# A float64 weight conversion in an attention and MLP kernel: from two byte-shifted loads to one load and integer steps

## The chip, the cores and the metric

The kernel runs on one core of a Trainium2 chip. The metric is the device time of one execution in microseconds; the profile's times come from one execution taken by the hardware profiler. A core has TensorE (PE: matmuls, and PEld for its weight loads), VectorE (DVE), ScalarE (ACT), GpSimd (POOL) and SyncE (SP, which here only starts transfers), each with its own queue of instructions in a fixed order, and 16 DMA engines that all queues share.

## The reference

Attention over 8 batches of 8 heads (576 rows of 64 numbers each, float32), in which scores more than tau below their row's largest are dropped, and then a two-layer MLP with an exact GELU over the 4608 rows of 512:

```python
scores = scale * np.matmul(q, k.transpose(0, 1, 3, 2))
thresh = np.max(scores, axis=-1, keepdims=True) - tau
scores = np.where(scores >= thresh, scores, -1000000000.0)
scores = scores - np.max(scores, axis=-1, keepdims=True)
attn = np.exp(scores)
attn = attn / (np.sum(attn, axis=-1, keepdims=True) + 1e-09)
x = np.matmul(attn, v)          # then (B,H,S,D) -> (B*S, H*D)
...
h = x @ w_in                    # 512 x 2048
g = 0.5 * h * (1.0 + erf(h * inv_sqrt2))
return (g @ w_out).astype(np.float32)   # 2048 x 512
```

q, k and v are float32. The two weights are float64: each number arrives as two 32-bit words, and the kernel has to make float32 of 2 x 1,048,576 of them.

## The kernel before

**Stages.** The kernel goes through 32 pairs of heads (`NP`), four pairs to a batch, and five chunks of query rows to a pair. One step of its main loop (line 845) takes one pair and one chunk; I call it a slot. The first batch is the early phase, slots 0 to 19: its list of slots (line 817) first takes chunks 0 and 1 of all four pairs, then chunks 2, 3 and 4 of each. Chunks 0 to 3 have two score tiles of 128 x 576, chunk 4 (the tails of both heads) has one. In the early phase PE also turns q and k (`turn_qk_early`) and the softmax output (`turn_p_early`) by matmuls, later DVE's transposes and DMAs do that. Behind the attention, PE fills in MLP blocks of 256 rows (`fill`, `block_steps`): layer one is L559, layer two L573. The last ten blocks are done at the end in five pairs by a Strassen scheme (L693).

**One early slot, in the order of the engines' queues.** PE makes the scores sc (L367), which need the two PSUM buffers that the slot before has freed. DVE finds the negative row maximum nmx (L379), POOL makes the threshold thr (L380), ACT the exponentials p (L382). DVE then masks p and sums it (L398). Conversion steps of the weights come next on DVE and ACT. POOL adds 1e-9 to the sums (L401). At the end of the slot DVE inverts them (den, L409), and ACT writes them on a diagonal, diag (L412). In the next slot PE multiplies p with diag (tr, L309), which divides and turns at once, and ACT copies the result out (pT, L317, L328; L321 and L333 for chunk 4). PE's xT (L484) weighs v with pT, and ACT copies that too (L493). Every second early slot up to slot 4 also has ACT copy the turned q and k (L283, L285, L292, L293, L296). From slot 10 on, PE does some 10 or 12 records of layer one (hT, L559) between scores and tr.

**The weights** are 32 pieces of 128 x 512 numbers, 16 of w_in and 16 of w_out. `load_piece` (line 139) starts the DMAs of one piece, twice: the piece as it is (raw, L156: 1024 words a row) and the same bytes moved by three (shifted, L158), so that a shifted word has the 28 bits of the number's fraction in place. Even pieces and the last two go to tiles of the pool xg, odd ones to the tile turned_p, which is idle in the early phase. Two pieces are started on SP before the loop (line 810), one each in slots 0 and 2 (line 891); after that each conversion that ends starts the next load, on POOL's queue.

`conversions` (line 161) is a generator that gives out the steps of a piece, and its yields are the nanoseconds that a step is counted as. For each piece: DVE masks the exponent bits (L177), ACT scales and rebiases them into a float32 power of two (L178), DVE cuts the fraction out of the shifted words (L185), puts the sign to the power (L187), and multiplies both (L189). The first two steps run one piece ahead. `convert(ns)` (line 196) runs steps until their yields have used up what it was given: nothing in slot 0, 2000 in slots 1 and 2, 3800 in each further slot of the early phase (line 910), and some of it between nmx and p (line 876). The last two pieces wait until the others are done.

Of the kernel before, what the change touches and what calls it, by code (L numbers as in the profile page):

```python
# [8 lines left out]
FP32 = mybir.dt.float32  # L9
U32 = mybir.dt.uint32  # L10
U8 = mybir.dt.uint8
AF = mybir.ActivationFunctionType
ALU = mybir.AluOpType
# [5 lines left out]
def kernel(  # L19
# [28 lines left out]
    nc = tc.nc  # L48
# [4 lines left out]
    P = 128  # L53
# [24 lines left out]
    const = ctx.enter_context(tc.tile_pool(name="const", bufs=1))  # L78
# [4 lines left out]
    xg = ctx.enter_context(tc.tile_pool(name="xg", bufs=7))  # L83
    op = ctx.enter_context(tc.tile_pool(name="op", bufs=2))
# [17 lines left out]
    pd = [turned_p[:, e, :, :, :].rearrange("p h b i -> p (h b i)") for e in range(2)]  # L102
# [8 lines left out]
    q_scale = const.tile([P, 1], FP32, name="q_scale")  # L111
    tau_eff = const.tile([P, 1], FP32, name="tau_eff")

    rebias = const.tile([P, 1], FP32, name="rebias")
    nc.vector.memset(rebias, -8.0 * 896 * 2 ** 20)

    w_in_sb = [const.tile([P, d_ff], FP32, name=f"w_in{c}") for c in range(N_DM)]
    w_out_sb = [const.tile([P, d_model], FP32, name=f"w_out{j}") for j in range(N_DF)]

# [4 lines left out]
    for _ in range(3):  # L124
# [3 lines left out]
    PIECE = 512  # L128
    pieces = [(w_in_sb[c][:, f:f + PIECE], moe_w_in[c * P:(c + 1) * P, f:f + PIECE])
              for f in range(0, d_ff, PIECE) for c in range(N_DM)]  # L130
# [3 lines left out]
    LATER = 2  # L134
    raws = []
    loaded = [0]
    converted = [0]

    def load_piece(eng=nc.gpsimd):
        if loaded[0] == len(pieces):  # L140
            return
        dst, src = pieces[loaded[0]]
        loaded[0] += 1
        if not wide:
            nc.sync.dma_start(dst, src)
            converted[0] += 1
            load_piece()
            return
        k = loaded[0] - 1
        if k % 2 and k < len(pieces) - LATER:  # L150

            room = pd[k // 2 % 2].bitcast(U32)
            raw, shifted = room[:, 0:2 * PIECE], room[:, 2 * PIECE:4 * PIECE]
        else:
            raw, shifted = (xg.tile([P, 2 * PIECE], U32, tag="x", name=s) for s in ("raw", "shifted"))
        eng.dma_start(raw, src.bitcast(U32))  # L156
        n = 8 * PIECE - 4
        eng.dma_start(shifted.bitcast(U8)[:, 0:n], src.bitcast(U8)[:, 3:3 + n])  # L158
        raws.append((dst, raw, shifted))

    def conversions():

        vec = nc.vector
        ahead = []  # L170
        while raws or ahead:
            if raws:
                dst, raw, shifted = raws.pop(0)
                hi = raw.rearrange("p (f w) -> p f w", w=2)[:, :, 1]
                top = shifted.rearrange("p (f w) -> p f w", w=2)[:, :, 0]
                power = gp.tile([P, PIECE], U32, tag="g", name="power")
                vec.tensor_scalar(power, hi, 0x7FF00000, None, op0=ALU.bitwise_and)  # L177
                nc.scalar.activation(power, power, AF.Relu, bias=rebias, scale=8.0)  # L178
                ahead.append((dst, hi, top, dst.bitcast(U32), power))
                yield 340  # L180
            if len(ahead) == LATER and converted[0] == len(pieces) - LATER:
                yield None
            if len(ahead) == 2 or not raws:
                dst, hi, top, mant, power = ahead.pop(0)
                vec.tensor_scalar(mant, top, 0x0FFFFFFF, 0x10000000, op0=ALU.bitwise_and, op1=ALU.bitwise_or)  # L185
                yield 340
                vec.scalar_tensor_tensor(power, hi, 0x80000000, power, op0=ALU.bitwise_and, op1=ALU.bitwise_or)  # L187
                yield 720
                vec.scalar_tensor_tensor(dst, mant, 2.0 ** -28, power.bitcast(FP32), op0=ALU.mult, op1=ALU.mult)  # L189
                load_piece()  # L190
                converted[0] += 1
                yield 700

    conv = {"steps": None, "debt": 0.0}

# [162 lines left out]
    def scores(p, i):  # L358
        s = st[p]
        n = 1 if i == NC else 2  # L360
        sc = s["sc", i] = [ps.tile([P, 2, 512], FP32, tag="sc", name="sc", bufs=2) for _ in range(n)]
        for h in range(2):
            for e in range(n):
                rows = slice(0, P) if i == NC else slice(e * D, (e + 1) * D)
                lhsT = s["q_tail"] if i == NC else s["qT"][rows, i * P:(i + 1) * P]
                at = h * HALF + (TAIL if p < EARLY and e == 0 else 0)
                nc.tensor.matmul(  # L367
                    sc[e][:, h, 0:HALF], lhsT=lhsT, rhs=s["kT"][rows, at:at + HALF], start=True, stop=True)
# [150 lines left out]
    def gelus(left):  # L519


        while len(late) > left:
            g, j, hT = late.pop(0)
            t = gp.tile([P, 2, TOK], FP32, tag="g", name="g")
            if hold[0]:
                nc.scalar.copy(t, hT)
                held.append((g, j, t))
            else:
                gelu(g, j, t, hT)
# [82 lines left out]
    vec = nc.vector  # L612
# [193 lines left out]
    load_early(2)  # L806
    for t in q_tail + v_sb:
        nc.gpsimd.memset(t, 0.0)
    for _ in range(2):
        load_piece(nc.sync)  # L810
    turn_qk_early(0)
    load_v_early(0)
# [32 lines left out]
    for n in range(len(slots) + WEIGH + 1):  # L845
        p, i = slots[n] if n < len(slots) else divmod(n, SLOTS)
        early = p < EARLY
        last = slots[n - 1] if 0 < n <= len(slots) else None
        if p < NP:
            scores(p, i)  # L850
            softmax_head(p, i)
            if p < HP - 1 and i == 0:
                turn_qk_early(p + 1)
        elif n == len(slots):
            ext = weights_in()
        gelus(0)
        if n == BATCH:
            gelus_held()
        table()
        for args in due:  # L860
            weigh_v(*args)
        due = []
        if p > EARLY and i == WEIGH:
            for lo, hi in (0, WIDE), (WIDE, S):
                weigh_v(p - 1, lo, hi)
            if p == NP:
                divide(p - 1)
        owed += (goal(n) - goal(n - 1)) * BLK_NS * (PARTS[i] if not early and p < NP else 1.0)
        if early:
            fill(owed, tokens)  # L870
            owed = 0.0
            table()
        if last and last[0] < EARLY and last[1] < NC:
            turn_p_early(*last)
        if early and n > 2:
            convert(0, 700 if i == NC else 1)
        if p < NP:
            softmax_tail(p, i)
        if p < NP and not early:
            turn_p(p, i)  # L880
        if p < NP and not early:
            if i == 2:
                regroup(p, 1)
            if i > 2:
                regroup(p, i)
            if i == NC:
                divisors(p)
        if last and last[0] < EARLY and last[1] == NC:
            turn_p_early(*last)
        if p < 2 and i == 0:  # L890
            load_piece()
            load_v_early(p + 2)
        if p == 1 and i == NC:
            load(HP)
        if n == BATCH - 3:
            load(HP + 1)
        if n == BATCH:
            for t in pd_tail + [turned_p[:, e, h, :, :] for e in range(2) for h in range(2)]:
                nc.gpsimd.memset(t[:, NB:4 * KR, :], 0.0)
        if EARLY < p < NP and i == DIVIDE:  # L900
            divide(p - 1)
        if p >= HP and i == 1 and p + 2 < NP:
            loads = load_steps(p + 2)
        if p >= HP:
            next(loads, None)
        if p >= HP and i == 1 and p + 1 < NP or p == HP - 1 and i == 2:
            scale_q(p + 1)
        if p >= HP - 1 and i == 2 and p + 1 < NP:
            turn_qk(p + 1)
        convert(0 if n == 0 else 2000 if n < 3 else 3800 if n < BATCH - 1 else 1e9)  # L910
        if early:
            diagonal(p, i)
        if not early:
            lag[0] = 2 if p < NP else 0
            fill(owed, tokens)
            owed = 0.0
        if last and last[0] < EARLY:
            if last[1] == 1:
                due.append((last[0], 0, TOK))
            if last[1] == NC:  # L920
                due.append((last[0], TOK, S))
        if n == START - 1:
            tokens = TOK
        elif n == BATCH + 1:
            tokens = S
        elif p > EARLY and i == DIVIDE and p % HP == 0 or p == NP and i == WEIGH:
            tokens = p // HP * S
            leaving += [n for n in AWAY if n in x_blk and (n + 1) * TOK <= tokens]
        elif leaving and i < 2:
            put_away(leaving.pop(0))  # L930
# [34 lines left out]
```

## Time and profile before

| | us |
|---|---|
| median of 6 runs | 1380.1 (1378.96 to 1381.46) |
| the profiled execution | 1378.96 |
| its span in the profile | 1377.1 |
| PE busy in the span | 1358.3 (99%) |
| DVE busy | 892.5 (65%) |
| ACT busy | 639.7 (46%) |
| POOL busy | 436.1 (32%) |
| read from memory / written to it | 72.73 MB / 12.52 MB |

The page cuts the span into 40 slices of 34 us; a digit gives the busy tenths of a slice. Groups are instructions of one line and shape, with the total and the mean of one, and the idle time ahead of them on their engine. On a timeline each row is a start, a length, an engine and an instruction; brackets hold the idle time ahead of it and what ended that. A float32 matmul shows as two records. L numbers are lines of the kernel before.

### The profile page before, as it was taken

What the parts mean: (1) busy time and instruction counts of PE and PEld (TensorE: products, weight loads), DVE (VectorE), ACT (ScalarE), POOL (GpSimd) and SP (SyncE); (2) the same over time, 40 slices, a digit from 0 to 9 for tenths busy, and PEclk for the clock granted to TensorE, in tenths of its full rate; (3) what the DMA queues carried; (4) which work ended last, traced back from release to release, by engine and by line L of the source; (5) the groups of instructions that cost most, each with busy time, mean ns of one, the idle gap of its engine ahead of it and who ended that gap; (6) DMA issues with size and microseconds to landing.
All of it is one profiled execution on the core that took longest, in us unless ns stands there. A gap on an engine that the chain in (4) does not pass through costs nothing.

```text
span 1377.1 us, 20235 instructions
## 1 busy us (share of the span) xinstructions
PE 1358.3 (99%) x6734; PEld 968.1 (70%) x6734; DVE 892.5 (65%) x1740; ACT 639.7 (46%) x1160; POOL 436.1 (32%) x896
## 2 busy tenths in 40 slices
PE   8899999999999999999999999999999999999999
PEld 6677556466466566575475475588888888888887
DVE  7998777878888888888888888763142241241330
ACT  7766537458358358357367366241240230330420
POOL 5453444454554555555555541100000000000000
PEclk9899999999999999999999999999999999999999
DMA  8987376577687687787787775500000001001000
GB/s 290 318 293 232 87 160 141 138 177 168 156 180 166 157 203 160 165 214 160 167 216 154 172 181 112 111 0 8 23 1 27 20 1 50 12 0 54 9 8 23
DMA packets 215095, 169.19 MB, mean 123 GB/s; under 512 B 114177, under 2 KB 199489, under 8 KB 214993
## 3 DMA queue, kind: packets, MB, share of 16 engines
q1 hardware_dynamic: 191040, 112.84, 36.5%
q0 software_dynamic: 23520, 54.77, 12.9%
q8 instruction: 55, 0.90, 0.3%
q14 instruction: 48, 0.39, 0.1%
q10 hardware_dynamic: 432, 0.30, 0.1%
HBM read 72.73 MB, written 12.52 MB: 62 GB/s over the span
## 4 chain that ended last, share of the span: by engine, by line
PE 95%; DMA 2%; DVE 2%; ACT 1%; SPq 1%; issue 0%; POOL 0%; ACTq 0%; POOLq 0%; DVEq 0%
PE bank L693 35%; PE hT L559 17%; PE o_ps L573 17%; PE sc L367 13%; PE xT L484 11%; PE tr L309 2%; DMA turned_p<-in_moe_w_in_dram 1%; DMA raw<-in_moe_w_in_dram 1%; DVE nmx L379 0%; DVE power L187 0%; ACT p L382 0%; SPq L249 0%; DVE p L398 0%; SPq L253 0%; DVE power L177 0%
## 5 line engine op out<-in xcount | busy, mean ns | idle before, releaser
L382 ACT ACTIVATE p<-sc,nmx 128x576 f32<-128x576 f32 x288 | 202.1, 739 | 267.1 <-DVE nmx L379 266.9
L398 DVE SCALAR_TENSOR_TENSOR p<-sc,thr,p 128x576 f32<-128x576 f32 x288 | 225.3, 816 | 60.5 <-ACT p L382 59.3
L379 DVE TENSOR_REDUCE nmx<-sc 128x1 f32<-128x576 f32 x288 | 205.6, 751 | 62.1 <-PE sc L367 61.2
L559 PE MATMUL hT<-x,w_in 128*128 128x256 f32 x1024 | 241.1, 385 | 0.0
L573 PE MATMUL o_ps<-w_out,g 128*128 128x512 f32 x512 | 236.7, 603 | 0.0
L559 PEld LDWEIGHTS hT<-x,w_in 128*128 128x128 f32 x1024 | 189.5, 190 | 49.2 <-issue 23.5
L380 POOL TENSOR_SCALAR thr<-nmx,tau_eff 128x1 f32<-128x1 f32 x288 | 89.7, 311 | 388.4 <-DVE nmx L379 388.0
L573 PEld LDWEIGHTS o_ps<-w_out,g 128*128 128x128 f32 x512 | 93.0, 189 | 110.2 <-issue 108.6
L484 PE MATMUL xT<-pT,v 128*64 128x256 f32 (+1 forms) x1280 | 163.8, 409 | 0.0
L367 PE MATMUL sc<-kT,qT 64*128 64x288 f32 x960 | 155.9, 430 | 2.4 <-DVE p L398 1.9
L445 DVE STREAM_TRANSPOSE turned_p<-p 128x1152 f32<-128x1152 f32 x112 | 154.4, 1378 | 3.9
L367 PEld LDWEIGHTS sc<-kT,qT 64*128 64x128 f32 x960 | 89.1, 187 | 75.3 <-issue 64.3
L484 PEld LDWEIGHTS xT<-pT,v 128*64 128x64 f32 x1280 | 89.1, 137 | 72.1 <-issue 13.2
L693 PE MATMUL bank<-x,w_in 128*128 128x256 f32 x480 | 116.7, 379 | 0.0
L693 PE MATMUL bank<-w_out,unit 128*128 128x256 f32 x520 | 115.5, 379 | 0.0
L234 POOL DMA_DIRECT2D v<-in_v_dram x208 | 111.3, 538 | 4.3 <-issue 2.3
L693 PEld LDWEIGHTS bank<-w_out,unit 128*128 128x128 f32 x520 | 98.8, 190 | 13.4
L693 PEld LDWEIGHTS bank<-x,w_in 128*128 128x128 f32 x480 | 91.2, 190 | 12.8 <-issue 0.5
L693 PE MATMUL bank<-v,unit 128*128 128x256 f32 x320 | 82.1, 379 | 0.0
L225 POOL DMA_DIRECT2D q<-in_q_dram x104 | 71.0, 687 | 10.0 <-issue 8.9
L693 PE MATMUL bank<-unit,turned_p 128*128 128x256 f32 x320 | 73.1, 379 | 0.0
L532 ACT ACT_TABLE_LOAD x56 | 71.8, 1283 | 1.0
(161 smaller groups left out, 1489.7 us busy)
## 6 DMA issues: line engine op xcount, KB each, us to landing
pT<-turned_p SPq DMA_DIRECT2D x448, 160.0 KB, 3.6
pT<-pd_tail SPq DMA_DIRECT2D x112, 80.0 KB, 3.0
q<-in_q_dram POOLq DMA_DIRECT2D x104, 72.0 KB, 3.5
k<-in_k_dram POOLq DMA_DIRECT2D x104, 72.0 KB, 2.8
inv<-turned SPq DMA_DIRECT2D x56, 128.0 KB, 3.9
v<-in_v_dram POOLq DMA_DIRECT2D x156, 40.0 KB, 3.2
x<-x SPq DMA_DIRECT2D x10, 512.0 KB, 4.3
raw<-in_moe_w_out_dram POOLq DMA_DIRECT2D x9, 512.0 KB, 4.3
```

The costliest lines, as they stand in the source:

```text
L234: eng.dma_start(t[r:P:4, e, 0:n, :], rows[:, r * KR:r * KR + n, :])
L367: nc.tensor.matmul(sc[e][:, h, 0:HALF], lhsT=lhsT, rhs=s["kT"][rows, at:at + HALF], start=True, stop=True)
L379: nc.vector.tensor_reduce(nmx[:, e:e + 1], sc, axis=AXIS.XY, op=ALU.max, negate=True)
L380: nc.gpsimd.tensor_scalar(thr[:, e:e + 1], nmx[:, e:e + 1], -1.0, tau_eff, op0=ALU.mult, op1=ALU.subtract)
L382: nc.scalar.activation(w[:, e * S:(e + 1) * S].rearrange("p (h s) -> p h s", h=2), sc, AF.Exp, bias=nmx[:, e:e + 1], scale=1.0)
L398: nc.vector.scalar_tensor_tensor(row, sc[e][:, :, 0:HALF], thr[:, e:e + 1], row, op0=ALU.is_ge, op1=ALU.mult, accum_out=den[e])
L445: nc.vector.transpose(turned_p[:, :, i // 2, 0:NB, i % 2 * Q:(i % 2 + 1) * Q], w.rearrange("p (e b i) -> p e b i", e=2, i=Q))
L484: nc.tensor.matmul(to, lhsT=s["v"][:, e, c, :], rhs=rhs, start=(c == 0), stop=(c == KR - 1))
L532: nc.scalar.activation(t, src, AF.Gelu)
L559: nc.tensor.matmul(hT[:, j % 2, :], lhsT=w_in_sb[c][:, j * P:(j + 1) * P], rhs=x_blk[n][:, c, :], start=(c == 0), stop=(c == N_DM - 1))
L573: nc.tensor.matmul(o[:, 0:d_model], lhsT=g[j][:, m * P:(m + 1) * P], rhs=w_out_sb[j], start=(j == 0), stop=(j == N_DF - 1))
L693: nc.tensor.matmul(to, lhsT=l, rhs=r, start=start and k == 0, stop=k == len(pairs) - 1, skip_group_check=not start)
```

## The change

Only one load is made for a piece, and the arithmetic changes. ACT scales the high words, read as float32, by 2^-112: that shifts the exponent by a constant and leaves the fraction. ACT also scales the low words, read as integers, by 2^-29: the top three bits, rounded, written into the destination tile. DVE shifts the first result left by three and clears its top bit, puts the sign in, and adds the second as an integer. [...] Both activations stand in the generator's step ahead, which now counts as nothing; the mask on DVE ahead of ACT and the tile rebias are gone. Odd pieces use four quarters of turned_p in place of two halves. Four pieces are started on SP before the loop and two each in slots 0 and 2.

```diff
@@ load_piece @@
-        k = loaded[0] - 1
-        if k % 2 and k < len(pieces) - LATER:
-            room = pd[k // 2 % 2].bitcast(U32)
-            raw, shifted = room[:, 0:2 * PIECE], room[:, 2 * PIECE:4 * PIECE]
+        if staged:
+            half, at = divmod(k // 2 % 4, 2)
+            raw = pd[half].bitcast(U32)[:, at * 2 * PIECE:(at + 1) * 2 * PIECE]
         else:
-            raw, shifted = (xg.tile([P, 2 * PIECE], U32, tag="x", name=s) for s in ("raw", "shifted"))
+            raw = xg.tile([P, 2 * PIECE], U32, tag="x", name="raw")
         eng.dma_start(raw, src.bitcast(U32))
-        n = 8 * PIECE - 4
-        eng.dma_start(shifted.bitcast(U8)[:, 0:n], src.bitcast(U8)[:, 3:3 + n])
-        raws.append((dst, raw, shifted))
+        raws.append((dst, raw))
@@ conversions @@
-                vec.tensor_scalar(power, hi, 0x7FF00000, None, op0=ALU.bitwise_and)
-                nc.scalar.activation(power, power, AF.Relu, bias=rebias, scale=8.0)
-                ahead.append((dst, hi, top, dst.bitcast(U32), power))
-                yield 340
+                nc.scalar.activation(power.bitcast(FP32), hi.bitcast(FP32), AF.Copy, bias=0.0, scale=2.0 ** -112)
+                nc.scalar.activation(dst.bitcast(U32), lo, AF.Copy, bias=0.0, scale=2.0 ** -29)
+                ahead.append((dst, hi, power))
+                yield 0
...
-                vec.tensor_scalar(mant, top, 0x0FFFFFFF, 0x10000000, op0=ALU.bitwise_and, op1=ALU.bitwise_or)
+                vec.tensor_scalar(power, power, 3, 0x7FFFFFF8, op0=ALU.logical_shift_left, op1=ALU.bitwise_and)
                 yield 340
                 vec.scalar_tensor_tensor(power, hi, 0x80000000, power, op0=ALU.bitwise_and, op1=ALU.bitwise_or)
                 yield 720
-                vec.scalar_tensor_tensor(dst, mant, 2.0 ** -28, power.bitcast(FP32), op0=ALU.mult, op1=ALU.mult)
+                vec.tensor_tensor(dst.bitcast(U32), power, dst.bitcast(U32), op=ALU.add)
                 load_piece()
                 converted[0] += 1
-                yield 700
+                yield 640
@@ main loop @@
-    for _ in range(2):
+    for _ in range(4):
         load_piece(nc.sync)
...
         if p < 2 and i == 0:
-            load_piece()
+            for _ in range(2):
+                load_piece()
             load_v_early(p + 2)
```

More of the change, by code (lines that the diff above doesn't have):

```diff
@@ L112 @@
     tau_eff = const.tile([P, 1], FP32, name="tau_eff")
-    rebias = const.tile([P, 1], FP32, name="rebias")
-    nc.vector.memset(rebias, -8.0 * 896 * 2 ** 20)
     w_in_sb = [const.tile([P, d_ff], FP32, name=f"w_in{c}") for c in range(N_DM)]
@@ L139, in load_piece @@
     def load_piece(eng=nc.gpsimd):
-        if loaded[0] == len(pieces):
+        k = loaded[0]
+        if k == len(pieces):
             return
-        dst, src = pieces[loaded[0]]
+        staged = k % 2 and k < len(pieces) - LATER
+        dst, src = pieces[k]
         loaded[0] += 1
@@ L172, in conversions @@
             if raws:
-                dst, raw, shifted = raws.pop(0)
-                hi = raw.rearrange("p (f w) -> p f w", w=2)[:, :, 1]
-                top = shifted.rearrange("p (f w) -> p f w", w=2)[:, :, 0]
+                dst, raw = raws.pop(0)
+                lo, hi = (raw.rearrange("p (f w) -> p f w", w=2)[:, :, i] for i in range(2))
                 power = gp.tile([P, PIECE], U32, tag="g", name="power")
-                vec.tensor_scalar(power, hi, 0x7FF00000, None, op0=ALU.bitwise_and)
-                nc.scalar.activation(power, power, AF.Relu, bias=rebias, scale=8.0)
-                ahead.append((dst, hi, top, dst.bitcast(U32), power))
-                yield 340
+                nc.scalar.activation(power.bitcast(FP32), hi.bitcast(FP32), AF.Copy, bias=0.0, scale=2.0 ** -112)
+                nc.scalar.activation(dst.bitcast(U32), lo, AF.Copy, bias=0.0, scale=2.0 ** -29)
+                ahead.append((dst, hi, power))
+                yield 0
             if len(ahead) == LATER and converted[0] == len(pieces) - LATER:
@@ L183, in conversions @@
             if len(ahead) == 2 or not raws:
-                dst, hi, top, mant, power = ahead.pop(0)
-                vec.tensor_scalar(mant, top, 0x0FFFFFFF, 0x10000000, op0=ALU.bitwise_and, op1=ALU.bitwise_or)
+                dst, hi, power = ahead.pop(0)
+                vec.tensor_scalar(power, power, 3, 0x7FFFFFF8, op0=ALU.logical_shift_left, op1=ALU.bitwise_and)
                 yield 340
```

## The prediction

> **What bounds the kernel.** I read the page's busy line and slices first: TensorE (PE) is busy 99% of the span, and PE, VectorE (DVE), ScalarE (ACT) and the DMA engines are all loaded in the first four slices (138 us), which hold every weight conversion.
>
> ```profile
> PE   8899999999999999999999999999999999999999
> ...
> DVE  7998777878888888888888888763142241241330
> ACT  7766537458358358357367366241240230330420
> ...
> PEclk9899999999999999999999999999999999999999
> DMA  8987376577687687787787775500000001001000
> ```
>
> The instruction lists of the two programs have the same matmuls in the same order. So the change can only alter PE's idle time and its granted clock, and only in those 138 us. The PE timeline there has the stalls (column in brackets: idle before, and what ended it):
>
> ```profile
> 22.27 1.53 PE L309 MATMUL tr<-diag,p 128*128 128x128 f32 x12 [1.02 <-ACT qT L283]
> ...
> 45.51 3.90 PE L309 MATMUL tr<-diag,p 128*128 128x128 f32 x20 [2.09 <-ACT diag L412]
> ...
> 52.82 2.42 PE L309 MATMUL tr<-diag,p 128*128 128x128 f32 x20
> ...
> 60.06 4.41 PE L309 MATMUL tr<-diag,p 128*128 128x128 f32 x20 [3.65 <-ACT diag L412]
> 64.39 1.86 PE L367 MATMUL sc<-kT,qT 64*128 64x288 f32 x8
> ...
> 130.16 2.42 PE L309 MATMUL tr<-diag,p 128*128 128x128 f32 x20 [1.54 <-ACT g L526]
> ```
>
> Up to 145 us the bracketed idle times add to 11.4 us, 2.3 of them before 12 us, where no weight is converted yet. The same 20 records take 2.42 us at 52.82 but 3.90 and 4.41 behind an idle PE, and the scores take 1.86 instead of 1.24: 1.5 + 2.0 + 0.6 = 4.1 us lost to the clock (granted 0.66 in 45 to 50 us, 0.53 in 60 to 66). Between 66 and 128 us PE has no recorded wait. So some 9 + 4 = 13 us are within the change's reach, 0.9%, and no more.
>
> I call one (pair, chunk) step a slot, numbered from 0; slots 0 to 19 are the early phase, and the first nmx of a slot on the DVE timeline is its start (slot 5 at 38.58, 6 at 44.73, 7 at 50.83, 8 at 59.43, 9 at 66.29 us). Slots 2 to 8 go at the pace of DVE and ACT, slots 9 to 17 at PE's (three slots, two full and one half, from the sc at 101.13 to that at 121.49: 20.4 us).
>
> **Part 1, the second load goes.** 32 loads of 0.51 MB leave a DMA that was busy over its full share in places. What it cost is DVE's wait for it:
>
> ```profile
> 17.38 0.43 DVE L177 TENSOR_SCALAR power<-turned_p 128x512 uint32<-128x512 uint32 x1 [1.22 <-DMA turned_p<-in_moe_w_in_dram]
> ...
> 57.34 0.43 DVE L177 TENSOR_SCALAR power<-turned_p 128x512 uint32<-128x512 uint32 x1 [1.63 <-DMA turned_p<-in_moe_w_in_dram]
> ...
> 111.42 0.45 DVE L177 TENSOR_SCALAR power<-raw 128x512 uint32<-128x512 uint32 x1 [1.02 <-DMA raw<-in_moe_w_out_dram]
> ```
>
> Five such waits (1.22, 0.23, 1.63, 1.02, 0.88) make 5.0 us. The last two fall in slots 15 and 16, under a busy PE, and are worth nothing. With eight single pieces in flight a piece has about three slots (20 us) to land against 8 us measured, so I let all five go; if a load were late after all, 1.6 us would come back. Of the 1.22 in slot 1 only 0.6 is won: the new DVE chain waits there for ACT, whose last copy ends at 16.0. SP still issues four weight DMAs of 0.5 MB ahead of v, so nothing behind them moves. POOL loses 32 issues of 0.55 us, but DVE waited for its thr only 0.3 us here and there: counted at nothing; were POOL's thr late once per slot it would be those 0.3.
>
> **Part 2, DVE per piece.** These groups carry the prices (count, then busy time and mean ns):
>
> ```profile
> L178 ACT ACTIVATE power<-power,rebias 128x512 uint32<-128x512 uint32 x32 | 22.9, 728 | 12.4 <-DVE power L177 12.3
> ...
> L187 DVE SCALAR_TENSOR_TENSOR power<-raw,power 128x512 uint32<-128x512 uint32 x17 | 11.7, 686 | 0.4 <-ACT power L178 0.4
> ...
> L189 DVE SCALAR_TENSOR_TENSOR w_out<-w_out,power 128x512 f32<-128x512 uint32 x16 | 11.0, 690 | 0.4
> ...
> L177 DVE TENSOR_SCALAR power<-raw 128x512 uint32<-128x512 uint32 x17 | 7.3, 429 | 2.1 <-DMA raw<-in_moe_w_out_dram 1.9 <-DMA raw<-in_moe_w_in_dram 0.2
> ...
> L532 ACT ACTIVATE g<-g 128x512 f32<-128x512 f32 x6 | 3.2, 617 | 0.0
> ```
>
> On the timeline an independent successor starts 0.08 us before its predecessor's end, a dependent one 0.03 after it. Before: 0.34 (L177) + 0.34 (L185) + 0.72 (L187, L189 needs it) + 0.61 = 2.01 us a piece. After: the shift-and-mask 0.45 (0.42, and now the next step needs it), the sign step 0.72, the add 0.61 = 1.78. The add is the unknown. The program's list has it as a custom instruction over 128x1024 16-bit halves. Below, nearest in kind, stands a 512-word two-operand step, 0.69 (L189); a one-operand step of 512 words, 0.42 (L177), is the lowest row there is. Above, 1024 halves taken singly, like the 576 elements of L398 in 816 ns and the 1152 of L445 in 1378: by the slope (562 ns for 576) about 1.25. I take 0.69, since the halves are the same bytes in the same 512 words as L189's. [...] No row here shows a 16-bit step.
>
> The kernel deals conversions out by its own yields: 3.8 us a slot, formerly at 2.10 a piece, now at 1.70. So a slot gets 2.24 pieces instead of 1.81, and DVE's slot becomes nmx 1.32 + p 1.47 + den 0.07 + 2.24 x 1.78 = 6.84, where it was 2.86 + 1.81 x 2.01 = 6.50. **Each slot grows by 0.34 us; only the number of slots with conversions falls, from 19 to 16.**
>
> **Part 3, ACT per piece.** One activation with a bias tile (0.73, two of them 1.38, so 0.65 each in a row) becomes two with constants. By L532's g<-g (six in 3.23: 0.52 each in a row, 0.62 alone) that is 1.05 a piece. Its input is read at every second word, which no ACT row shows; the DVE rows with such input (L177, 0.42) show no sign of a penalty. Bounds: 0.84 (two at 0.42, the price of a 128x256 gelu, L737) to 1.38 (two like L178). I take 1.05: +0.40 a piece, +0.9 to +1.2 us a slot. All of it stands in ACT's queue between the last pT copy and diag, and diag is what PE waits for.
>
> **The slots, summed against this execution.**
> - Slots 1 to 8: six full-pace slots x 0.34 = +2.0; DMA waits 0.6 + 0.23 + 1.63 = -2.5. Slot 4 also carries the q/k copies (2.1 us) on ACT: after them pT ends near 37.4, two pieces at 39.5, and den, which now waits for ACT's second piece, comes near 39.9, so diag starts at 40.2 instead of 38.77; part is caught up: +1.0. PE still idles 2 to 3 us before slots 5's and 7's tr, so I keep both clock losses. Sum +0.5.
> - Slots 9 to 16: DVE needs 2 x 6.84 + 5.45 = 19.1 of PE's 20.4, formerly 18.1. ACT from tr's end to the next diag needs 0.8 + 2 x 1.05 + 0.4 = 3.3; PE between those tr has sc 1.17 + hT 2.16 = 3.3 in two slots of three, 7.1 in the third. Slot 10 has three pieces: 4.4 against 3.3, +1.1. Those of two pieces lose 0.1 to 0.5 each, four of them: +1.4. Sum +2.5. Before, diag was ready 0.9 to 3 us ahead of tr, which covered such delays.
> - Slots 17 to 19 have no conversions: the 1.54 at 130.16 goes, and most of the scores' bank wait before (1.94 against 1.24 at 121.49): -2.0. PE is next in line there, and can't catch up more.
>
> Sum +1.0: 1378.96 of the profiled execution (span 1377.1 and 1.9 around it) becomes 1380.0. The runs' median, 1380.1, lies 1.14 above that execution, so I forecast **1381.1 us**.
>
> **Rivals.**
> - *Faster:* DMA and clock were what counted. The 3.65 shrinks by the 1.63, PE is not slowed at 60 us (2.6), slots 17 and 18 give 2.0 and slots 9 to 16 lose nothing; the longer DVE slots cost 2.0: -1.6 - 2.6 - 2.0 + 2.0 = -4.2, **1375.9**. For it: both slow stretches start behind an idle PE. Against: 2.09 us of idle sufficed at 45.51, and idle of that size stays. [...]
> - *Slower by ACT's queue:* the conversions ahead of diag become the bound in the slots that give ACT only 3.3 us: 6 slots x 0.9 = 5.4, slot 4's 1.0 and a third slow stretch 1.5, less 2.0: +5.9, **1386.0**. It decides once a piece costs ACT more than 1.05. For it: PE waits for diag already (6.5 us). Against: ACT has 17.3 us of work in 20.4.
> - *Slower by the add:* at 1.25, 0.56 x 2.24 = 1.25 a slot: 7.5 in slots 3 to 8, then 22.9 against 20.4 per three slots, 6.6 in slots 9 to 16, with the forecast's other terms: +12 to +15, **1393**. Against: the words are 512.
> - *No effect* beyond earlier conversions is the forecast itself.
>
> **Chances.** 0.2% (2.8 us) is about what a measurement of this kernel can tell from no change. Forecast 0.40, faster rival 0.24, ACT 0.26, add 0.10: faster 0.24, same 0.40, slower 0.36. Alone the forecast spans 1377.4 to 1382.8; the range runs from just under the faster rival to just above ACT's, 1375.0 to 1387.0, which leaves the slow add out.
>
> **What would show it.** The new ACT pair at 0.62 each, shift 0.42, add 0.69; no DVE wait on a weight DMA; slots 5 to 8 at 6.8 us; DVE and ACT without conversions from about 120 us; a PE wait for diag near 80 us, none at 130. Wrong would be: a granted clock of 1.0 throughout 45 to 66 us (faster rival), ACT waits in most tr after 70 us (ACT), an add over 1 us.

## The result and the profile after

The changed kernel takes 1384.4 us (median of 17 runs, 1381.95 to 1385.69), the kernel before beside it 1379.7 us. The ratio is 1.0028, 95% interval 1.0022 to 1.0035: slower, by 0.28%. I had forecast 1381.1, no difference to be measured; the nearest rival in time was ACT's queue, 1386.0. The profiled execution took 1386.16 us, span 1384.1; it is longer than all 17 timed ones, so the two profiles differ by 7.2 us where the medians differ by 4.7.

The page of the changed kernel, busy tenths in slices of 34 us: VectorE (DVE) and ScalarE (ACT) are nearly as busy as before in the first four slices, and the DMA is no longer full in them (mean share 0.69 in 34 to 68 us, 1.06 before).

```profile
PE   8899999999999999999999999999999999999999
...
DVE  6987677788888888888888888764142232241330
ACT  7886537457457448358366366241140230330420
...
PEclk9999999999999999999999999999999999999999
DMA  8641266667777787687787776500000001001000
```

The instructions of a piece, by line and shape (line numbers are five lower than before from L177 on: L172 and L173 are the two activations, L180 the shift, L182 the sign, L184 the add, L404 den, L407 diag, L393 p, L304 tr, L362 sc):

```profile
L180 DVE TENSOR_SCALAR power<-power 128x512 uint32<-128x512 uint32 x32 | 13.5, 422 | 6.3 <-ACT power L172 6.3
...
L182 DVE SCALAR_TENSOR_TENSOR power<-raw,power 128x512 uint32<-128x512 uint32 x17 | 11.8, 692 | 0.6
L172 ACT ACTIVATE power<-raw 128x512 f32<-128x512 f32 x17 | 11.7, 690 | 0.0
L184 DVE CUSTOM_DVE_ANT_0 w_out<-power,w_out 128x1024 uint16<-128x1024 uint16 x16 | 11.0, 690 | 0.9
...
L173 ACT ACTIVATE w_out<-raw 128x512 uint32<-128x512 uint32 x9 | 6.2, 684 | 0.0
```

The three DVE steps cost what was reckoned. DVE no longer waits for any weight DMA; it now waits 6.3 us for ACT, of which 2.05 (this row) fall in slot 12 and 0.95 in slot 13:

```profile
96.53 0.43 DVE L180 TENSOR_SCALAR power<-power 128x512 uint32<-128x512 uint32 x1 [2.05 <-ACT power L172]
```

The PE timeline, idle time before a record and its releaser in brackets:

```profile
22.70 2.51 PE L304 MATMUL tr<-diag,p 128*128 128x128 f32 x12 [0.97 <-ACT qT L278]
...
42.82 2.42 PE L304 MATMUL tr<-diag,p 128*128 128x128 f32 x20 [1.00 <-ACT diag L407]
...
49.58 3.83 PE L304 MATMUL tr<-diag,p 128*128 128x128 f32 x20 [2.83 <-ACT diag L407]
...
62.83 3.47 PE L304 MATMUL tr<-diag,p 128*128 128x128 f32 x20 [2.13 <-ACT diag L407]
...
83.53 1.52 PE L304 MATMUL tr<-diag,p 128*128 128x128 f32 x10 [1.17 <-ACT diag L407]
85.78 1.94 PE L362 MATMUL sc<-kT,qT 64*128 64x288 f32 x8 [0.73 <-DVE p L393]
...
134.06 2.32 PE L304 MATMUL tr<-diag,p 128*128 128x128 f32 x20
```

The wait of 1.54 at 130 us is gone, as foreseen; there are new ones at 42.82 and around 84 us, where before had none. To see where the time went I compare when PE starts the tr of the same slot in both executions. The lateness is +0.77 us at slot 0, +1.72 at slot 8, **+6.37 at slot 16** and +3.72 at slot 19. So slots 9 to 16 cost 4.65, and the end gives 2.65 back. Behind that, between 145 and 170 us, this execution lost another 3.3 to a slow clock (0.86 granted there, 1.00 before: the scores took 2.99 us for 1.94, the ten records behind them 6.84 for 4.56); other runs of the same place show losses from 0 to 3.3, so this is chance.

### The profile page after: what moved, and what is told of

Its sections match the earlier page's. It is cut to its first block, busy times and chain, and to the rows that moved or that the text cites. A ratio compares the mean times of both kernels' runs of the same rounds, so it can differ in the third digit from the quotient of the medians.

```text
span 1384.1 us, 20244 instructions
## 1 busy us (share of the span) xinstructions
PE 1363.6 (99%) x6734; PEld 970.0 (70%) x6734; DVE 884.1 (64%) x1707; ACT 654.9 (47%) x1192; POOL 415.4 (30%) x864
## 4 chain that ended last, share of the span: by engine, by line
PE 95%; DVE 2%; ACT 2%; issue 1%; DVEq 0%; ACTq 0%
PE bank L688 35%; PE o_ps L568 17%; PE hT L554 16%; PE sc L362 13%; PE xT L479 11%; PE tr L304 2%; DVE power L182 1%; DVE nmx L374 1%; ACT p L377 0%; DVE p L393 0%; ACT power L172 0%; DVE power L180 0%; ACT pT L312 0%; ACT diag L407 0%; PE idle L122 0%
## 5 line engine op out<-in xcount | busy, mean ns | idle before, releaser
L393 DVE SCALAR_TENSOR_TENSOR p<-sc,thr,p 128x576 f32<-128x576 f32 x288 | 225.3, 816 | 60.9 <-ACT p L377 59.2
L362 PE MATMUL sc<-kT,qT 64*128 64x288 f32 x960 | 157.6, 433 | 3.2 <-DVE p L393 2.6
L362 PEld LDWEIGHTS sc<-kT,qT 64*128 64x128 f32 x960 | 90.1, 188 | 76.6 <-issue 64.4
```

The source lines that it names most:

```text
L362: nc.tensor.matmul(sc[e][:, h, 0:HALF], lhsT=lhsT, rhs=s["kT"][rows, at:at + HALF], start=True, stop=True)
L393: nc.vector.scalar_tensor_tensor(row, sc[e][:, :, 0:HALF], thr[:, e:e + 1], row, op0=ALU.is_ge, op1=ALU.mult, accum_out=den[e])
```

## The experiments

Three theories. **Queue**: the two activations of each piece, 1.14 us and not 1.05, stand ahead of diag in ACT's queue. **Pace**: a slot gets 2.24 pieces instead of 1.81, too much DVE work, whoever shares it. **Clock**: slow stretches of PE by chance. Each run was timed beside the kernel before; the table gives the ratio to it, and the lateness of PE's tr against before's profiled execution (13.15, 68.50, 120.06 and 139.23 us).

| run | pieces a slot | slots with three | tr slot 0 | slot 8 | slot 16 | slot 19 | ratio (95%) |
|---|---|---|---|---|---|---|---|
| changed kernel | 2.24 | 5, 10, 14 | +0.77 | +1.72 | +6.37 | +3.72 | 1.0028 (1.0022 to 1.0035) |
| E1 slower pace | 1.81 | none | +0.23 | -2.28 | -2.23 | -1.54 | 0.9991 (0.9983 to 1.0000) |
| E2 before, one load | 1.81 | none | +0.49 | -4.62 | -3.14 | -1.59 | 0.9993 (0.9985 to 1.0002) |
| E4 one activation | 2.24 | 5, 10, 14 | +1.35 | -0.03 | +4.37 | +1.72 | 1.0013 (1.0003 to 1.0023) |
| E5 before, faster pace | 2.24 | 4, 8, 13 | +1.22 | +3.82 | +9.91 | +7.26 | 1.0050 (1.0037 to 1.0064) |
| E7 middle pace | 2.00 | none | +0.66 | -1.34 | -0.05 | -1.06 | 0.9995 (0.9985 to 1.0004) |
| E9 by stage | 1.59 to 2.35 | none | +0.75 | -4.13 | -2.13 | -2.88 | 0.9979 (0.9968 to 0.9990) |
| E10 halves, 3400 | 2.00 | none | +0.56 | -2.42 | -1.08 | -2.15 | 0.9978 (0.9969 to 0.9987) |
| E11 halves, 3800 | 2.24 | 5, 10, 14 | +0.23 | -1.45 | +5.78 | +3.13 | 1.0008 (0.9999 to 1.0018) |
| E12 by stage and halves | 1.59 to 2.35 | none | +1.31 | -4.92 | -3.14 | -3.64 | 0.9969 (0.9959 to 0.9979) |

("Slots with three" counts the shift steps between the nmx of one slot and of the next; the rest of a third piece can fall into the next slot.) E3, E8 and E15 are told of below.

**E1: the pace of before.**

```diff
-        convert(0 if n == 0 else 2000 if n < 3 else 3800 if n < BATCH - 1 else 1e9)
+        convert(0 if n == 0 else 2000 if n < 3 else 3080 if n < BATCH - 1 else 1e9)
```

> The changed kernel with 3080 instead of 3800 ns of conversion steps dealt to a slot: at 1.70 a piece that is 1.81 pieces a slot, as many as the kernel before did. Theory queue (the two activations of each piece stand ahead of diag in ACT's queue, 1.14 us a piece where 1.05 was reckoned, and PE waits for diag): the slots with three pieces go, those with two stay, so 3 of the 4.4 us lost in slots 9 to 16 come back, and 2.2 are given up at the end, where conversions run to slot 19 again: 1382.5 to 1384, against 1384.4 of the changed kernel and 1379.7 of the one before. Theory pace (the slot is too full of DVE work, whoever does it): DVE's slot falls to 2.86 + 1.81 x 1.78 = 6.08 us, under the 6.50 of before, so slots 3 to 8 gain 0.7 each and slots 9 to 16 lose nothing: 1377 to 1380. Theory clock (the slow stretches of PE are by chance and the rest is a sum of them): 1384.

Measured 1379.7 us, 0.9991. One number, and the loss is gone: this is pace's range, 3 us better than queue's. Of the 8.6 us between the two at slot 16 (+6.37 against -2.23), 0.5 are there at slot 0 already, and 1.6 are a slow tr and a slow sc in slot 2 that only the changed kernel's profile has (22.70: 2.51 for 1.53, and 1.82 for 1.24; 0.66 granted in 22 to 27 us, 1.00 before); the other 6.5 go with how many pieces a slot takes. PE has no wait between 60 and 98 us, and the stall at the end is back, because conversions run to slot 19 again:

```profile
45.67 4.05 PE L304 MATMUL tr<-diag,p 128*128 128x128 f32 x20 [2.47 <-ACT diag L407]
...
58.85 3.89 PE L304 MATMUL tr<-diag,p 128*128 128x128 f32 x20 [2.13 <-ACT diag L407]
...
98.83 1.94 PE L362 MATMUL sc<-pd_tail,qT 64*128 64x288 f32 x8 [0.28 <-DVE p L393]
...
119.65 1.94 PE L362 MATMUL sc<-pd_tail,qT 64*128 64x288 f32 x8 [0.40 <-DVE p L393]
...
128.29 2.42 PE L304 MATMUL tr<-diag,p 128*128 128x128 f32 x20 [1.50 <-ACT g L521]
```

**E2: the kernel before with one load.**

```diff
-        eng.dma_start(shifted.bitcast(U8)[:, 0:n], src.bitcast(U8)[:, 3:3 + n])
-        raws.append((dst, raw, shifted))
+        raws.append((dst, raw))
...
-                top = shifted.rearrange("p (f w) -> p f w", w=2)[:, :, 0]
+                top = raw.rearrange("p (f w) -> p f w", w=2)[:, :, 0]
```

> The kernel before without its second load: the fraction is cut out of the low words of the first load, which leaves out the true fraction but keeps every other instruction. It measures what one load alone is worth. By the prediction's sum the waits of DVE for the weight DMAs in slots 1 to 8, 2.5 us, go and the clock losses stay: 1377.2, 0.9982 of the kernel before. Rival, the DMA is hidden anyway and ACT and DVE set the slots: 1379.7. Rival, DMA and clock were what counted (idle before the tr in 60 us under 2 us, no slow stretch there): 1375 to 1376.

Measured 1380.2 beside 1381.2, 0.9993: -1.0 us with an interval of -2.1 to +0.3, so the rival "hidden anyway" is not excluded; 1377.2 (0.9982) lies just outside, 1376 farther. DVE's waits for weight DMAs are gone (5.0 us before), and at slot 8 PE is 4.6 us ahead, but it gives that back: 1.5 in slots 9 to 16, and in slot 17 the wait for g grows from 1.54 to 2.31 us with a slow tr behind it (3.43 for 2.42).

```profile
57.69 2.42 PE L307 MATMUL tr<-diag,p 128*128 128x128 f32 x20 [1.94 <-ACT diag L410]
...
127.01 3.43 PE L307 MATMUL tr<-diag,p 128*128 128x128 f32 x20 [2.31 <-ACT g L524]
```

**E3: den and diag ahead of the slot's conversions.**

```diff
+        if early:
+            diagonal(p, i)
         convert(0 if n == 0 else 2000 if n < 3 else 3800 if n < BATCH - 1 else 1e9)
-        if early:
-            diagonal(p, i)
```

> The changed kernel with den and diag ordered ahead of the slot's dealt conversions: ACT makes diag as soon as den is there, and the conversions' activations follow it. Theory queue: PE's waits for diag (7.8 us up to 165 us) mostly go, slots 9 to 16 are back at the pace of before: 1378 to 1380.5. The price would be DVE waiting for POOL's sum ahead of den, which conversions hid: below 0.5 us a slot. Theory pace: nothing is taken from DVE, its slot stays at 6.8 us or grows by that wait, 1384 to 1387. Theory clock: 1384.

Measured 1390.0 us, 1.0065 (1.0052 to 1.0078): worse than either theory said. PE's waits for diag fall from 7.8 us to 0.3, as queue had it, and the time grows all the same. The waits of DVE, and then of PE, from 12 to 145 us (total, times, longest):

```profile
DVE power L180 <- ACT power L172: 7.1, 5, 3.3
DVE den L404 <- POOL den L396: 6.4, 18, 0.4
```

```profile
PE sc L362 <- DVE p L393: 7.7, 6, 2.5
```

DVE waits for POOL's sum ahead of nearly every den, which the conversions used to cover, and now it is the masked p that comes late. The wait only moved, with 6.4 us of DVE time lost on top, and PE ran slowly behind some of the new waits too (the xT at 69.80 took 4.51 us, where 2.38 is usual).

**E4: one activation left out.**

```diff
-                nc.scalar.activation(dst.bitcast(U32), lo, AF.Copy, bias=0.0, scale=2.0 ** -29)
...
-                vec.scalar_tensor_tensor(power, hi, 0x80000000, power, op0=ALU.bitwise_and, op1=ALU.bitwise_or)
+                vec.scalar_tensor_tensor(dst.bitcast(U32), hi, 0x80000000, power, op0=ALU.bitwise_and, op1=ALU.bitwise_or)
...
-                vec.tensor_tensor(dst.bitcast(U32), power, dst.bitcast(U32), op=ALU.add)
+                vec.tensor_tensor(power, power, dst.bitcast(U32), op=ALU.add)
```

> The changed kernel without the second activation of a piece: DVE's three steps stay in number, shape and order, the last adds into a tile nobody reads, and the low three bits of each fraction are left out. ACT per piece falls from 1.14 to about 0.6 us, below the 0.65 of before. Theory queue: 4 to 5 us come back, 1379.5 to 1380.5. Theory pace: DVE's slot stays at 6.84, so at most 1 us comes back, 1383.5 to 1384.5. Theory clock: 1384.

Measured 1382.9 us, 1.0013: 0.15% or 2 us come back, between the theories. The table says where: from slot 0 to slot 8 it loses 2.3 us less than the changed kernel (1.6 of that is the slow stretch in slot 2 that only the changed kernel's profile has), and from slot 8 to slot 16 both lose nearly the same, 4.4 and 4.65. So ACT's half of the pair costs something in the first slots, where ACT also copies q and k, and next to nothing where the loss is. How much of the median it carries stays uncertain, since the two intervals just touch. Why it is so little in slots 9 to 16, ACT itself shows. Its timeline in the changed kernel at the end of slots 10 and 11 (idle and releaser in brackets):

```profile
81.95 0.70 ACT L173 ACTIVATE w_out<-turned_p 128x512 uint32<-128x512 uint32 x1
83.07 0.40 ACT L407 ACTIVATE diag<-ident,den 128x128 f32<-128x128 f32 x1 [0.42 <-DVE den L404]
...
89.40 0.70 ACT L407 ACTIVATE diag<-ident,den 128x128 f32<-128x128 f32 x2 [1.07 <-DVE den L404]
```

and the same places in E4:

```profile
78.62 0.70 ACT L172 ACTIVATE power<-turned_p 128x512 f32<-128x512 f32 x1
81.30 0.40 ACT L406 ACTIVATE diag<-ident,den 128x128 f32<-128x128 f32 x1 [1.98 <-DVE den L403]
...
87.62 0.69 ACT L406 ACTIVATE diag<-ident,den 128x128 f32<-128x128 f32 x2 [2.22 <-DVE den L403]
```

Ahead of diag ACT is idle, in the changed kernel too: den is what is late. Without the second activation ACT just waits longer. Den stands in DVE's queue behind all conversion steps of the slot, and here is slot 10 of the changed kernel on DVE, three shifts and all:

```profile
75.77 0.74 DVE L374 TENSOR_REDUCE nmx<-sc 128x1 f32<-128x576 f32 x1
76.43 0.42 DVE L180 TENSOR_SCALAR power<-power 128x512 uint32<-128x512 uint32 x1
...
79.86 0.43 DVE L180 TENSOR_SCALAR power<-power 128x512 uint32<-128x512 uint32 x1 [0.94 <-ACT power L172]
...
81.76 0.42 DVE L180 TENSOR_SCALAR power<-power 128x512 uint32<-128x512 uint32 x1
82.21 0.69 DVE L182 SCALAR_TENSOR_TENSOR power<-raw,power 128x512 uint32<-128x512 uint32 x1
82.82 0.15 DVE L404 RECIPROCAL den<-den 128x1 f32<-128x1 f32 x1
```

The wait of 0.94 is no price of the second activation: E4 has it at the same place, 0.92, and the 2.05 and 0.95 of slots 12 and 13 as 2.03 and 0.94. ACT comes to the piece only after the pT copies, which wait for PE's tr: in the changed kernel's slot 10 the copies start at 77.60 and 78.50, each after 0.31 us of waiting for tr, and the piece's first activation at 79.14; in slot 12 the first copy waits 2.07 us for tr, and the activation starts at 95.81. But DVE's time it is all the same. From nmx to nmx, slots 9 to 11 take DVE 19.9 us and slots 12 to 14 22.1; PE took 20.1 and 19.9 for them before (tr to tr: 68.50, 88.62, 108.47).

**E5: the old steps at the new pace**, 4700 instead of 3800 in line 910 of the kernel before.

> The kernel before with its two loads and its old arithmetic, but 4700 instead of 3800 ns dealt to a slot: at 2.10 a piece 2.24 pieces a slot, the pace that the change brought with it. Theory pace (what costs is the number of pieces a slot has to take, whatever they are made of): DVE's slot grows to 2.86 + 2.24 x 2.01 = 7.36 us, 0.86 more than before in slots 3 to 8, +5; slots 9 to 16 lose the 2 to 4 of the changed kernel, and the end gives 3 back because conversions are done by slot 16: +4 to +6, ratio 1.003 to 1.0045. Theory new steps (the loss lies in the new arithmetic: ACT's two activations and DVE's waits for them): the old steps at the new pace lose little and gain the early end: -3 to +1, 0.998 to 1.001.

Measured 1388.1 us, 1.0050: pace, a little above its range, and "new steps" is out. The old arithmetic at 2.24 pieces a slot is worse than the new one by 0.22%, 3.0 us, which is what the longer DVE chain would make it: 2.24 x (2.01 - 1.78) = 0.52 us a slot, 3.1 in slots 3 to 8. It is not shown that the chain alone does it: E5 also keeps the second load, and DVE waits 3.9 us for weight DMAs there, 2.86 of them in slot 15. PE's waits for diag are 11.4 us up to 145 us, against 6.5 before and 7.8 in the changed kernel.

**E7: the pace between**, 3400 in place of 3800 in the changed kernel.

> The changed kernel with 3400 ns, 2.00 pieces a slot, between the 1.81 that gave 0.9991 and the 2.24 that gave 1.0028. If the cost goes by DVE work per slot, it is linear in the pace: 1.0005 to 1.0015. If it is a threshold (single slots that get a third piece): 0.9985 to 0.9995, as at 1.81. If it is already the full loss: 1.0025.

Measured 0.9995 (0.9985 to 1.0004), as at 1.81, and just under the range for a linear cost. So most of the cost comes above two pieces. At 3400 ns every slot from 3 to 15 takes two pieces and none three; slot 10 lasts 5.5 us from nmx to nmx, with three shifts in the changed kernel 7.1:

```profile
72.15 0.74 DVE L374 TENSOR_REDUCE nmx<-sc 128x1 f32<-128x576 f32 x1
...
76.52 0.43 DVE L180 TENSOR_SCALAR power<-power 128x512 uint32<-128x512 uint32 x1 [0.41 <-ACT power L172]
...
77.59 0.16 DVE L404 RECIPROCAL den<-den 128x1 f32<-128x1 f32 x1
```

Of the 1.6 us by which den comes later in the changed kernel, 1.1 are the third shift and sign, and 0.5 the longer wait for ACT. In slots 5 and 14 the third shift alone makes den 0.4 later than in a slot of two. One restriction: the intervals of 1.81 and 2.00 overlap, so a slope between them stays possible; E9 below speaks for one in the slots that go at DVE's pace.

**E8: four pieces in flight**, at 3080 ns.

```diff
-    for _ in range(4):
+    for _ in range(2):
         load_piece(nc.sync)
...
-            for _ in range(2):
-                load_piece()
+            load_piece()
```

> The changed kernel at 3080 ns with four pieces in flight instead of eight: two started on SP ahead of the loop and one each in slots 0 and 2. It measures what the four further loads are worth. If a load then comes late in slots 1 to 8, DVE waits for DMA 1 to 2 us in all come back: 1.000 to 1.001. If one load per piece is enough by itself (the kernel before without its second load had no DVE wait on DMA worth speaking of and stood at 0.9993): 0.9985 to 0.9995, no different from eight.

Measured 0.9993 (0.9983 to 1.0004), against 0.9991 with eight: no difference that shows. DVE waits for no weight DMA here either (ACT does once, 0.4 us). So what made the DMA late was the second load, not the number of pieces in flight.

**E9: dealt by what a slot has room for.**

```diff
-        convert(0 if n == 0 else 2000 if n < 3 else 3800 if n < BATCH - 1 else 1e9)
+        convert(0 if n == 0 else 2000 if n < 3 else (2700 if n < 8 else 4000 if i == NC else 3200) if n < BATCH - 1 else 1e9)
```

> The changed kernel with the conversions dealt by what a slot has room for: 2700 ns (1.59 pieces) in slots 3 to 7, 3200 (1.88) in later full slots and 4000 (2.35) in chunk-4 slots, whose softmax is half as long. If DVE's work sets slots 3 to 7 below two pieces as well, 0.4 us less in each of five slots: 0.9975 to 0.998, against 0.9991 at 1.81 pieces everywhere. If only a third piece in a slot costs (2.00 pieces gave 0.9995, 2.24 gave 1.0028), there is nothing left to gain from fewer: 0.9988 to 0.9998.

Measured 1377.6 us, 0.9979 (0.9968 to 0.9990), which is what was expected if fewer than two pieces gain as well in slots 3 to 7. It speaks against a cost of the third piece alone, but does not exclude it: the interval reaches that theory's range too, and overlaps E1's and E7's. In slots 3 to 7 the slot goes at DVE's pace, and PE's wait ahead of the tr at 45 us falls to 1.55 us, from 2.47 in E1, after which the tr takes its usual 2.42 us. E6, with 3500 ns in the later full slots and 4600 in the chunk-4 slots, gave no result: its queues would have waited for each other (a deadlock).

**E10 and E11: the slot's amount in two halves, den and diag between them**, at 3400 ns (1700 and 1700) and at the changed kernel's 3800:

```diff
-        convert(0 if n == 0 else 2000 if n < 3 else 3800 if n < BATCH - 1 else 1e9)
+        convert(0 if n == 0 else 2000 if n < 3 else 1900)
         if early:
             diagonal(p, i)
+        if n > 2:
+            convert(1900 if n < BATCH - 1 else 1e9)
```

> The changed kernel at 3400 ns a slot, dealt in two halves with den and diag between them: the first half covers POOL's sum, the second no longer stands ahead of diag. At 3400 undivided it was 0.9995. If PE's waits for diag in slots 5 and 7 (2.13 us each, with 4 us of slow clock behind them) come from the conversions ahead of diag, 3 to 5 us go: 0.996 to 0.9975. If DVE's work is what is late there, the wait only moves from diag to p, as with diag ahead of all conversions: 0.999 to 1.001.

> The same halves with diag between them at the pace of the changed kernel, 3800 ns. The order alone is changed. Theory pace: the three slots with three pieces stay, 1.002 to 1.004 as undivided (1.0028). Theory queue, in the form that is left (diag ahead of all conversions made DVE wait 0.36 us for POOL in every slot, which hid the gain): 0.999 to 1.0005.

Measured 0.9978 (0.9969 to 0.9987) and 1.0008 (0.9999 to 1.0018): 0.17% better than undivided at 3400, where the intervals just overlap, and 0.20% at 3800, where they are apart. Both results lie between the ranges of the two theories. So order counts after all, but by den and not by ACT: the first half covers POOL's sum, the second no longer stands ahead of den. In E10 the two waits of 2.13 us for diag become

```profile
44.80 2.42 PE L304 MATMUL tr<-diag,p 128*128 128x128 f32 x20 [0.46 <-ACT diag L407]
...
48.66 2.57 PE L362 MATMUL sc<-pd_tail,qT 64*128 64x288 f32 x8 [1.44 <-DVE p L393]
...
58.80 2.42 PE L304 MATMUL tr<-diag,p 128*128 128x128 f32 x20 [0.73 <-ACT diag L407]
...
61.90 1.94 PE L362 MATMUL sc<-kT,qT 64*128 64x288 f32 x8 [0.68 <-DVE p L393]
```

Part of the wait moves to p, and neither tr is slow (the scores at 48.66 and the xT behind them are, by 1.6 us). At 3800 the three slots with three pieces stay and PE is still 5.78 us late at slot 16. It loses 7.23 us in slots 9 to 16, more than the undivided kernel, although den comes early: now the scores of slot 12 wait for slot 11's p.

```profile
82.67 2.99 PE L362 MATMUL sc<-kT,qT 64*128 64x288 f32 x8 [1.62 <-DVE p L393]
85.59 5.11 PE L479 MATMUL xT<-pT,v 128*64 128x320 f32 x20
```

Some 3.3 of the 7.23 are slow records behind this wait (2.99 for 1.94, 5.11 for 2.91). So the halves win in slots 1 to 8 (E10 is 1.0 us ahead of E7 there, and level in slots 9 to 16); in slots 9 to 16 of E11 the wait only changes its name, and what costs there is DVE's time per slot. Order and pace are two costs, and the pace is the larger one: 0.33% from 2.24 to 2.00.

**E15: halves at 3080 ns** (1540 and 1540).

> The changed kernel at the pace of the kernel before, 3080 ns or 1.81 pieces a slot, in two halves with den and diag between them; undivided it was 0.9991. If the order by itself is worth 0.17%, as at 3400 (0.9978 against 0.9995) and 3800 (1.0008 against 1.0028): 0.997 to 0.998. If it is worth something only while slots are full: 0.9985 to 0.9995.

Measured 1376.7 us, 0.9977 (0.9967 to 0.9987): the order is worth 0.14% at the old pace, about as much, with intervals that overlap.

**E12: both, by stage and in halves** (`ns = 2700 if n < 8 else 4000 if i == NC else 3200`, half of it ahead of diag and half behind).

> The changed kernel with both measures that gained by themselves: the amounts by stage (2700 ns in slots 3 to 7, 3200 in full and 4000 in chunk-4 slots; alone 0.9979) and each slot's amount in halves with den and diag between them (at 3400 in all slots 0.9978, against 0.9995 undivided). If the two take away different waits, they add: 0.996 to 0.997. If both take away the same ones, the PE waits for diag in slots 5 to 7 and the slow clock behind them, little is left: 0.9975 to 0.998.

Measured 1376.0 us beside 1380.7, **0.9969** (0.9959 to 0.9979): the fastest here. The two measures add only in part; that they do at all is not certain, since the interval meets those of E9, E10 and E15.

## Why the prediction was near, and where it failed

Against the kernel before, the sum said +1.0 us and the medians show +4.7. The result lies above the forecast's own span (1377.4 to 1382.8); the stated range holds it because it was drawn around the rivals too. One reading was off without consequence: the idle times before 12 us add to 2.1 us, not 2.3.

- **DVE per piece.** Right: 422, 692 and 690 ns, against 0.42, 0.69 and 0.69; the add was sized by the row it is nearest to, and the slow-add rival is out. Slots 5 to 8 last 6.76, 6.92, 6.33 and 7.15 us (6.8 foreseen).
- **ACT per piece.** The first mis-sized term: 1.05 taken, 1.14 measured. In a row the activations start 0.57 us apart and take 0.69 alone, where I had used L532's 0.52 and 0.62, from dense input. The error is 0.2 us a slot on ACT (2.24 x 0.09); E4, which takes off the whole second activation, wins 2 us in all.
- **The second load.** The waits went as foreseen: taken at -2.5, by E2 -1.0 (-2.1 to +0.3). In E2's profile PE gained more than that in slots 1 to 8, 5.1 us, of which 2.9 are shorter waits (4.7 us in all, 7.6 before) and 2.2 faster records, but lost 3.0 again by slot 19. The sum had no term for giving it back.
- **Slots 1 to 8.** +0.5 taken, +0.95 measured, with 1.6 in it from a slow tr and a slow sc in slot 2 (22.70: 2.51 for 1.53) that E4, E7, E10 and E11 don't have. Without them it would be -0.6, so that the two are near is luck.
- **Slots 9 to 16: the step that failed.** +2.5 taken, +4.65 measured, and put down to the wrong engine. The prediction let "DVE needs 2 x 6.84 + 5.45 = 19.1 of PE's 20.4" pass as room to spare, and sought the loss in ACT's 3.3 us between tr and diag. The 20.4 is that of slots 15 to 17; for slots 9 to 11 and 12 to 14 PE took 20.1 and 19.9. DVE took 19.9 and 22.1 for them in the changed kernel. What the 19.1 lacked are DVE's waits for ACT's power, 0.94 and 3.0 us, which the sum put at nothing. And the room is an average over three slots, while den and p are due in every single one: slot 10, with its third shift and sign and the longer wait, has its den 1.6 us later than with two. PE's lateness grows by 2.7 us from the tr of slot 9 to that of slot 11, and by 1.55 from slot 11 to slot 14. Whole steps and the waits among them had to be counted, slot by slot, on the engine that makes den and p. How much of slots 12 to 14 is the third shift of slot 14 and how much the waits is not shown.
- **Slots 17 to 19.** -2.0 taken, -2.65 measured.
- **What is within reach.** I said that only the first 138 us can change. The wait ahead of the scores at about 160 us, 1.58 or 1.59 us, is the same in every timeline here, and what the records behind it lose is 0 to 3.3 us.
- **Rivals.** ACT's queue came nearest in time, in the main for the wrong reason: with half of ACT's work per piece gone (E4) the ratio is still 1.0013, while fewer pieces at the full ACT price (E1, E7) leave no loss. Its condition, over 1.05 us a piece, was met at 1.14, and it still didn't decide. E3, aimed at it too, changes DVE's order as well and tells less. The faster rival lacked the full clock: 0.83 and 0.82 granted in 50 to 60 and 60 to 66 us.

In sum: at the pace of before the change gains about 0.1% (E1), which is at the edge of what can be told; the 0.28% loss is that of the new yields. Counting a piece at 1.70 instead of 2.10 gave a slot 2.24 pieces, more than DVE has time for in some of them. E1, E5 and E7 show this. That PE's wait for diag is a wait for DVE's den is shown by ACT's idle time ahead of diag; that it is not den's place alone is shown by E11, where p is late instead. What stays open is what each slot adds, how much of the loss ACT's second activation carries, and how much of E1's gain is the load and how much the shorter DVE chain: E1 and E2 can't be told apart.

## What to carry to other kernels

A budget per step is spent in whole units: count how many slots get one unit more, not the average, add the waits inside the unit, and look what stands behind it in that queue. Follow the late instruction back one more step than the releaser named at the bottleneck: PE waited for ACT's diag, but ACT sat idle for DVE's den. When work is made cheaper, don't let the same budget pack more of it in; where a small instruction that others wait for stood behind all of the filler, it was worth 0.14 to 0.20% here to put it in the middle, behind what covers its own wait and ahead of the rest.

## What the runs showed of the chip

**The clock after an idle PE.** A tr of 20 records takes 2.42 us. Behind a single idle time of up to 1.55 us it always did (E9 at 45.28); in E3, behind two close together, 1.15 and 0.26 us, one took 4.41. Behind 1.83 us and more it took 3.1 to 4.4 in 17 of 18 cases (the other is the 1.94 in E2, above). This is a count over these runs and no threshold: a tr of 12 records took its usual 1.53 us behind 2.25 us of idle time in E3, and 2.51 behind 0.97 in the changed kernel.

```profile
45.28 2.42 PE L304 MATMUL tr<-diag,p 128*128 128x128 f32 x20 [1.55 <-ACT diag L407]
...
56.99 3.98 PE L304 MATMUL tr<-diag,p 128*128 128x128 f32 x20 [1.83 <-ACT diag L407]
```

The scores are caught by less, but not each time. In the changed kernel, behind the 1.58 or 1.59 us that all timelines have there:

```profile
162.16 2.99 PE L362 MATMUL sc<-kT,qT 64*128 64x288 f32 x8 [1.58 <-DVE p L393]
```

and in E9:

```profile
155.56 1.94 PE L362 MATMUL sc<-kT,qT 64*128 64x288 f32 x8 [1.58 <-DVE p L393]
```

The granted clock in 145 to 170 us was 0.86 in the changed kernel; in the kernel before, whose scores also took 1.94 us, behind 1.59, it was 1.00. In E11 the 1.62 us wait at 82.67 (above) cost about as much: the xT behind it took 5.11 us, against 2.91 in E10. So the effect varied from run to run: slow records followed idle times of 1.58 and 1.62 us in some executions, and in others the usual ones followed the same 1.58.

**ACT over every second word.** An activation with constants over 512 numbers, each second word, takes 0.69 us alone and 0.57 in a row; a dense one, the gelu L532 of the kernel before, 0.62 and 0.52. The two differ in their function too, so that the stride makes the difference is not shown. On DVE the shift over dense words and the old mask over every second word are alike, 422 and 429 ns.
